# Attention's stores of x and the loads of the rests on ScalarE's queue, and raw bits of weight tiles 1 to 4 in the places of later tiles

## Chip, cores and metric

One core of a Trainium2 chip. The metric is the device time of one execution, in microseconds (us).

## The reference

Linear attention feeds a SwiGLU layer, and this a bilinear layer. Shapes: q, k and v are (4, 8, 576, 64); each layer has 2304 tokens, model width 512 and inner width 1536. All is float32.

```python
q_s = softmax(q, axis=-1)              # exp(q - max) / (sum + 1e-9)
k_s = softmax(k, axis=2)               # the same along the sequence
kv = np.einsum('bhsd,bhse->bhde', k_s, v)
x = np.einsum('bhsd,bhde->bhse', q_s, kv)   # then (B*S, H*D) = (2304, 512)
g = x @ w_gate
x = (g * sigmoid(g) * (x @ w_val)) @ w_out
x = ((x @ w_a) * (x @ w_b)) @ w_out2
```

## The kernel before

**Tiles.** Tokens go in five blocks: the first 512 positions of each of the four batches, and a fifth block with the 64 left over of each batch ("the rests"). The order is layer 0 with blocks 0, 1, 2, 4, 3, then layer 1 with blocks 0 to 4. The inner width is cut into NF = 12 tiles f. For each block and f there are two up products (`up`, lines 646 to 659; for the very first `ups`, line 639), the gate on ScalarE and VectorE (`gated`, lines 665 to 670) and the down product (`down`, lines 681 and 684). The down product of f - 1 comes after the up products of f.

**float32 in three passes.** Each operand is split in a high part, a cast to fp32r (ScalarE, line 293), and a low part, the difference (VectorE or GpSimd, line 287); three matmuls stand for one product.

**Weights.** Weights come as 64-bit numbers and are read as pairs of 32-bit words. A tile f of a layer has parts of the gate (or a), the value (or b) and the output matrix. `convert` loads the raw words of half a tile in three DMAs (lines 331 and 336) and turns them into float32: line 353 or 355, 357 (ScalarE, in place on the low words), 359, 362 and 365 (VectorE), 370 (GpSimd as a rule, the last that reads the raw words), then the split to the weight tile w. The raw words of a half tile are 6 KB in each partition; in layer 0 they have three places (`wr0`, `wr1`, `xraw`), in layer 1 two. Tile 0 is loaded by part instead of by half and uses the same three. Weight tile f of a layer lives in place `w{f}` of 12 KB in each partition; there are 12. Attention units of batches 0 and 1 use the places `w8` to `w11` for k, q and v until the weights of tiles 8 to 11 are written there.

**Attention.** `attend(b, g)` makes x for two heads of batch b (16 units). Batch 0 runs first; its rests come in six DMAs (`load_rests`, line 388). In batches 1 to 3 each unit loads its own rests (line 466). x of batch 0 stays in SBUF. For batches 1 to 3 x goes to DRAM: ScalarE copies it to `ob` (line 596) and SyncE stores it (line 597, 256 KB). The rests of all batches are copied (line 603) and stored as well (line 604, 32 KB). `next_x` (line 614) loads x again when its block comes.

**The order of the work.** All operations are put into a plan. It gives each a due time, counted back from TensorE's main line, and simulates the engines and the DMA queue with rough costs: at each step the operation that can start first goes next, and among those the one that is due first. The result is one order for each engine's queue. `load` chains all loads of inputs (`last_load`), so that they stand on SyncE's queue in the order of the program: start loads, weight tiles 1 and 2, attention unit (1, 0), tiles 3 and 4, unit (1, 1), and so on. An engine works its queue in order, so an instruction that waits holds all behind it. This is true of SyncE's DMAs too.

Of the kernel before, what the change touches and what calls it, by code (L numbers as in the profile page):

```python
# [9 lines left out]
U32 = mybir.dt.uint32  # L10
F32R = mybir.dt.float32r
AF = mybir.ActivationFunctionType
# [18 lines left out]
class Plan:  # L31
# [9 lines left out]
    BEGIN = 0.58  # L41
    SAME, HOP = 0.1, 0.17
    SLACK = 0.7
    DMA_START, DMA_END, DMA_RATE = 1.1, 0.95, 360e3
    TABLE = 1.3
    WINDOW = 10.24 / 3
    FAR = 1e9
# [47 lines left out]
    def prepare(self):  # L95

        ops = self.ops
        self.succ = [[] for _ in ops]
        for n, op in enumerate(ops):
            for d in op["deps"] | op["order"]:  # L100
                self.succ[d].append(n)
        self.due = [0.0] * len(ops)
        for n in reversed(range(len(ops))):
            op = ops[n]
            cost = op["cost"]
            if op["engine"] == "sync":
                cost += self.DMA_START + self.DMA_END + op["nbytes"] / self.DMA_RATE
            t = self.FAR
            for s in self.succ[n]:
                hop = self.hop(op["engine"], ops[s]["engine"], self.SLACK) if n in ops[s]["deps"] else 0.0  # L110
                t = min(t, self.due[s] - hop)
            t -= cost
            self.due[n] = t if op["wanted"] is None else min(t, op["wanted"])

    def order(self):


        ops, succ, due = self.ops, self.succ, self.due
# [31 lines left out]
        while len(done) < len(ops):  # L150
            best = None
            for engine, queue in ready.items():
                options = []
                for n, r in queue.items():
                    for b in ops[n]["allocs"]:
                        r = max(r, min(free_at(tag) for tag in b.tag))
                    if r < self.FAR and (ops[n]["engine"] == engine or better_here(n, r)):
                        options.append((max(r, port_at(n, engine)), n))
                if options:
                    t = max(free.get(engine, self.BEGIN), min(options)[0])  # L160
                    first = min((due[n], n) for r, n in options if r <= t + 0.02)
                    if best is None or (t, first) < best[:2]:
                        best = (t, first, engine, first[1])
            if best is None:
                raise RuntimeError("the plan is stuck")
            t, _, engine, n = best
            op = ops[n]
            for which, (e, *_) in enumerate(op["runs"]):
                del ready[e][n]
                if e == engine:  # L170
                    run[n] = which
            _, cost, _, port = op["runs"][run[n]]
            if port:
                port_free = t + cost
            for b in op["allocs"]:
                slot[b] = min(b.tag, key=free_at)
                holder[slot[b]] = b
            if op["table"] and op["table"] != table:
                table, t = op["table"], t + self.TABLE
            free[engine] = t + cost  # L180
            if engine == "sync":
                dma_free = max(dma_free, t + self.DMA_START) + op["nbytes"] / self.DMA_RATE
                end[n] = dma_free + self.DMA_END
            elif engine == "tensor":
                window = int(t / self.WINDOW)
                used[window] = used.get(window, 0.0) + cost
                full = used.get(window - 1, 0.0) > 0.3735 * self.WINDOW
                free[engine] = end[n] = t + cost * (1 if full else 2)
            else:
                end[n] = t + cost  # L190
            issued[n] = free[engine]
            done.append(n)
            for s in succ[n]:
                left[s] -= 1
                if not left[s]:
                    at = ops[s]["engine"]
                    is_ready(s, max([end[d] + self.hop(ops[d]["runs"][run[d]][0], at, self.HOP)
                                     for d in ops[s]["deps"]] + [issued[d] for d in ops[s]["order"]]))
# [13 lines left out]
def kernel(  # L212
# [24 lines left out]
    nc = tc.nc  # L237
    B, H, S, D = q.shape
    DM = H * D
    DFF = w_gate.shape[1]  # L240
    P = 128
    KD = DM // P
    NF = DFF // P
    R = 4
    SM = R * P
    SL = S - SM
# [5 lines left out]
    WC = 512  # L252

    const = ctx.enter_context(tc.tile_pool(name="const", bufs=1))
    wp = ctx.enter_context(tc.tile_pool(name="wp", bufs=1))
    xp = ctx.enter_context(tc.tile_pool(name="xp", bufs=1))
    hp = ctx.enter_context(tc.tile_pool(name="hp", bufs=2))
    sp = ctx.enter_context(tc.tile_pool(name="sp", bufs=2))
    op = ctx.enter_context(tc.tile_pool(name="op", bufs=2))
# [17 lines left out]
    def pool_us(n, streams=2):  # L277
        return (0, 0.14 + n / 1100, 0.15 + n / 449, 0.18 + n / 590)[streams]
# [14 lines left out]
        add("scalar", act_us(n), lambda: nc.scalar.copy(out=hi(), in_=src()), [src_key], [hi_key])  # L293
        pair(n, lo, src, lambda: hi().bitcast(F32), ALU.subtract, [src_key, hi_key], [lo_key], not psum, not psum)

    def dma(fn, nbytes, reads, writes, due=None, after=(), issue=0.475):
        return add("sync", issue, fn, reads, writes, due=due, nbytes=nbytes, after=after)


    last_load, last_x = [], []  # L300
# [1 line left out]
    def load(fn, nbytes, writes, issue=0.475):  # L302
        n = dma(fn, nbytes, [], writes, after=last_load, issue=issue)
        last_load[:] = [n]
# [3 lines left out]
    w_t, w_parts = {}, {}  # L308
    WR, AT = ("wr0", "wr1"), ("a0", "a1", "a2")
    RAW = WR + ("xraw",)  # L310
    TOP = 122880.0
    LEAST = 2.0 ** -15

    def convert(l, f, c, ms, c0, c1, spare):


        n, width = len(ms), c1 - c0
        name = f"{l}_{f}_{c}"
        raw = Buf(sp, [P, n, width, 2], U32, RAW if spare else WR, f"wr{name}")
        a = Buf(sp, [P, n, width], U32, AT, f"a{name}")  # L320
        if (l, f) not in w_t:
            w_t[l, f] = Buf(wp, [P, 6, WC], F32R, f"w{f}", f"w{l}_{f}")
            w_parts[l, f] = {m: [] for m in range(3)}
        w = w_t[l, f]
        parts = [(raw, x) for x in range(n)]
        for x, m in enumerate(ms):
            w_parts[l, f][m].append(c)

            def get(x=x, m=m):
                if m < 2:  # L330
                    nc.sync.dma_start(  # L331
                        out=raw()[:, x].rearrange("p (c n) t -> p c (n t)", n=P),
                        in_=mats[l][m][:, f * 2 * P:(f + 1) * 2 * P].rearrange(
                            "(c p) n -> p c n", p=P)[:, c0 // P:c1 // P, :])
                else:
                    nc.sync.dma_start(
                        out=raw()[:, x].rearrange("p n t -> p (n t)"),
                        in_=mats[l][m][f * P:(f + 1) * P, 2 * c0:2 * c1])

            load(get, P * width * 8, [(raw, x)])  # L340

        def low():
            return raw()[:, :, :, 0]

        def high():
            return raw()[:, :, :, 1]

        def part(t):
            return w().rearrange("p (m t) n -> p m t n", t=2)[:, ms[0]:ms[-1] + 1, t, c0:c1]
# [5 lines left out]
            other=("vector", dve_us(e, 2), lambda: nc.vector.tensor_scalar(  # L355
                out=a(), in0=high(), scalar1=0x7FFFFFFF, scalar2=None, op0=ALU.bitwise_and), True))
        add("scalar", act_us(e) + 0.08, lambda: nc.scalar.activation(  # L357
            out=low(), in_=low(), func=AF.Copy, scale=2.0 ** -29), parts, [(raw, "low")])
        add("vector", dve_us(e, 2), lambda: nc.vector.tensor_scalar(  # L359
            out=a().bitcast(F32), in0=a().bitcast(F32), scalar1=TOP, scalar2=LEAST,  # L360
            op0=ALU.min, op1=ALU.max), [a], [a], port=True)
# [7 lines left out]
        def whole(engine):  # L369
            engine.tensor_tensor(out=a(), in0=a(), in1=low(), op=ALU.add)  # L370

        add("gpsimd", pool_us(e), lambda: whole(nc.gpsimd), [a, (raw, "low")], [a],
            other=("vector", dve_us(e), lambda: whole(nc.vector), True))
        split(lambda: part(0), lambda: part(1), lambda: a().bitcast(F32), e, (w, (c, 0)), (w, (c, 1)), a)

    def convert_tile(l, f):
        for h in range(2):
            spare = l == 0 and f < NF - 2
            list(convert(l, f, h, [0, 1, 2], h * WC // 2, (h + 1) * WC // 2, spare))


    def rest(h):
# [2 lines left out]
    def load_rests(b, src, at):  # L385

        for h in range(HG):
            load(lambda h=h: nc.sync.dma_start(
                out=rests()[rest(h), at],
                in_=src[b, :, SM:S, :].rearrange("(g h) s d -> h s g d", h=HG)[h]),  # L390
                SL * KD * D * 8, [(rests, (at, h))], issue=0.65)

    def attend(b, g, xhl, due):

# [196 lines left out]
        if xhl is not None:  # L591
            split(lambda: xhl()[:, 0, g, :], lambda: xhl()[:, 1, g, :], px, SM,
                  (xhl, (0, g)), (xhl, (1, g)), px, psum=True)
        else:
            ob = Buf(op, [P, 512], F32, ("ob0", "ob1"), f"xs{u}")
            add("scalar", act_us(SM), lambda: nc.scalar.copy(out=ob(), in_=px()), [px], [ob])
            dma(lambda: nc.sync.dma_start(out=xd[0][b]()[:, g, :], in_=ob()), P * SM * 4,
                [ob], [(xd[0][b], g)])
        add("tensor", mm_us(SL), lambda: nc.tensor.matmul(
            py(), lhsT=kvbd(), rhs=qT()[:, SM:S], start=True, stop=True), [QTL, *BDS], [py],  # L600
            due=None if due is None else due + 1)
        oc = Buf(op, [P, 512], F32, ("ob0", "ob1"), f"xq{u}")
        add("scalar", act_us(SL), lambda: nc.scalar.copy(out=oc()[:, 0:SL], in_=py()), [py], [oc])
        dma(lambda: nc.sync.dma_start(out=xd[0][B]()[:, g, b * SL:(b + 1) * SL], in_=oc()[:, 0:SL]),
            P * SL * 8, [oc], [(xd[0][B], (g, b))])


    def new_xhl(l, i):
# [194 lines left out]
```

## Time and profile before

| | us |
|---|---|
| median of 3 runs | 1038.8 |
| lowest and highest | 1037.66, 1039.71 |
| profiled execution | 1037.9 |
| its span from the first to the last instruction | 1036.0 |

| engine | busy, us | share of the span |
|---|---|---|
| TensorE, matmuls | 977.9 | 94% |
| VectorE | 431.8 | 42% |
| ScalarE | 357.7 | 35% |
| GpSimd | 178.2 | 17% |

In the profile PE is TensorE, PEld its loading of weights, DVE VectorE, ACT ScalarE, POOL GpSimd, and SPq SyncE's queue, which issues DMAs. L331 is line 331 of the kernel. Names of tiles stand as output<-input, without their numbers. Shares of the whole span are means over stages that differ: the first 200 us, where weights are converted and batch 1 goes through attention beside the first block, and the rest.

### The profile page before, as it was taken

To read this page: it belongs to the slowest core of one execution; us is meant where nothing else is said; L and a number is where in the kernel's file an instruction comes from. 1 tells how busy PE (TensorE), PEld (TensorE's weight loads), DVE (VectorE), ACT (ScalarE), POOL (GpSimd) and SP (SyncE) were. 2 spreads that over 40 slices of the span, in tenths; PEclk is the share of its full clock that TensorE was granted. 3 is DMA by queue.
4 is the path that set the end of the run, shared out by engine and by line. 5 is a ranking of instruction groups with operands and counts; after the bars stand their busy time and mean duration, and the time that the engine had idled before them with its cause. 6 is when DMAs were issued, how large, how long until landed. Compare 5 with 4: busy or idle time off the path is not lost.

```text
span 1036.0 us, 12377 instructions
## 1 busy us (share of the span) xinstructions
PE 977.9 (94%) x4792; PEld 797.4 (77%) x4792; DVE 431.8 (42%) x758; ACT 357.7 (35%) x574; POOL 178.2 (17%) x156
## 2 busy tenths in 40 slices
PE   4777879999999999999999999999999999999997
PEld 3455656677778777799888788888888888888897
DVE  5876688633334333432665774131113112111211
ACT  4556565432334323422355543121112112111211
POOL 4543444301110101100145443000000000000000
PEclk9989989999999999999999999999999999999999
DMA  6445543311121111521133531020002000100100
GB/s 198 120 134 168 168 149 111 117 56 47 47 69 59 46 46 46 175 92 61 62 123 122 194 108 54 1 82 1 1 1 82 1 1 0 61 1 1 41 1 22
DMA packets 63876, 74.22 MB, mean 72 GB/s; under 512 B 12616, under 2 KB 51016, under 8 KB 62920
## 3 DMA queue, kind: packets, MB, share of 16 engines
q1 hardware_dynamic: 63816, 73.42, 22.4%
q8 instruction: 38, 0.62, 0.3%
q14 instruction: 22, 0.18, 0.1%
HBM read 60.29 MB, written 13.11 MB: 71 GB/s over the span
## 4 chain that ended last, share of the span: by engine, by line
PE 80%; DMA 6%; DVE 5%; SPq 3%; issue 2%; ACT 2%; POOL 2%; DVEq 0%; POOLq 0%; ACTq 0%
PE u L654 51%; PE acc L684 14%; PE acc L681 11%; DMA wr<-in_moe_w_out_dram 3%; PE kv L544 2%; POOL a L370 1%; DVE a L365 1%; SPq L331 1%; DVE h L287 1%; SPq L461 1%; PE xt L589 1%; PE kv L546 1%; PE qt L574 1%; DMA ut<-in_v_dram 1%; DMA x<-ob 1%
## 5 line engine op out<-in xcount | busy, mean ns | idle before, releaser
L654 PE MATMUL u<-xhl,w 128*128 128x512 f32 (+1 forms) x2856 | 621.9, 372 | 14.8 <-DVE w L287 12.6
L654 PEld LDWEIGHTS u<-xhl,w 128*128 128x128 f32 x2856 | 497.0, 189 | 110.6 <-DVE w L287 11.7
L668 DVE TENSOR_TENSOR s<-s,u 128x512 f32<-128x512 f32 (+1 forms) x120 | 76.1, 634 | 395.1 <-PE u L654 382.7
L681 PE MATMUL acc<-h,w 128*128 128x512 f32 (+1 forms) x720 | 167.6, 379 | 12.5 <-DVE h L287 10.7
L681 PEld LDWEIGHTS acc<-h,w 128*128 128x128 f32 x720 | 125.5, 190 | 42.3 <-DVE h L287 14.4
L684 PE MATMUL acc<-w,h 128*128 128x512 f32 x648 | 157.5, 391 | 0.1
L665 ACT ACTIVATE s<-u 128x512 f32<-128x512 f32 (+1 forms) x120 | 66.6, 555 | 262.0 <-PE u L654 255.2
L684 PEld LDWEIGHTS acc<-w,h 128*128 128x128 f32 x648 | 120.7, 188 | 26.2 <-DVE h L287 1.3
L293 ACT CAST h<-s 128x512 fp32r<-128x512 f32 (+1 forms) x120 | 69.1, 576 | 205.0 <-DVE s L668 204.7
L370 POOL TENSOR_TENSOR a<-a,wr 128x768 uint32<-128x768 uint32 (+1 forms) x49 | 99.4, 2033 | 205.0 <-DVE a L365 141.4
L287 DVE TENSOR_TENSOR h<-s,h 128x512 fp32r<-128x512 f32 (+1 forms) x119 | 84.3, 709 | 51.5 <-ACT h L293 51.3
L287 POOL TENSOR_TENSOR xhl<-xraw,xhl 128x512 fp32r<-128x512 f32 (+1 forms) x5 | 6.0, 1202 | 337.9 <-ACT xhl L293 240.9
L365 DVE SCALAR_TENSOR_TENSOR a<-wr,a 128x768 uint32<-128x768 uint32 (+1 forms) x49 | 52.4, 1077 | 0.5
L353 ACT ACTIVATE a<-wr 128x768 f32<-128x768 f32 (+1 forms) x38 | 33.7, 888 | 45.0 <-DMA wr<-in_moe_w_out_dram 34.9
L293 ACT CAST w<-a 128x768 fp32r<-128x768 f32 (+1 forms) x49 | 39.9, 818 | 23.2 <-POOL a L370 19.8
L357 ACT ACTIVATE wr<-wr 128x768 uint32<-128x768 uint32 (+1 forms) x49 | 43.8, 893 | 10.3 <-DMA wr<-in_moe_w_out_dram 10.3
L359 DVE TENSOR_SCALAR a<-a 128x768 f32<-128x768 f32 (+1 forms) x49 | 36.0, 739 | 18.8 <-ACT a L353 18.3
L287 DVE TENSOR_TENSOR w<-a,w 128x768 fp32r<-128x768 f32 (+1 forms) x38 | 38.3, 1021 | 8.5 <-ACT w L293 8.5
L567 POOL TENSOR_TENSOR ua<-ua,st 128x576 f32<-128x576 f32 x8 | 9.2, 1154 | 122.4 <-DVE st L566 122.4
L362 DVE TENSOR_SCALAR a<-a 128x768 uint32<-128x768 uint32 (+1 forms) x49 | 27.6, 572 | 0.8
L287 POOL TENSOR_TENSOR w<-a,w 128x768 fp32r<-128x768 f32 (+1 forms) x11 | 22.9, 2080 | 19.6 <-ACT w L293 19.6
L697 DVE COPY ob<-acc 128x512 f32<-128x512 f32 (+1 forms) x20 | 12.7, 636 | 27.9 <-DMA out_dram<-ob 19.9
(94 smaller groups left out, 439.2 us busy)
## 6 DMA issues: line engine op xcount, KB each, us to landing
wr<-in_moe_w_out_dram SPq DMA_DIRECT2D x46, 256.0 KB
xraw<-x SPq DMA_DIRECT2D x7, 1024.0 KB
wr<-in_moe_w_a_dram SPq DMA_DIRECT2D x24, 256.0 KB
wr<-in_moe_w_b_dram SPq DMA_DIRECT2D x24, 256.0 KB
wr<-in_moe_w_gate_dram SPq DMA_DIRECT2D x22, 256.0 KB
wr<-in_moe_w_val_dram SPq DMA_DIRECT2D x22, 256.0 KB
x<-ob SPq DMA_DIRECT2D x16, 256.0 KB
out_dram<-ob SPq DMA_DIRECT2D x16, 256.0 KB
```

Of the source, the lines that this page charges most:

```text
L287: engine.tensor_tensor(out=out(), in0=x(), in1=y(), op=op)
L293: add("scalar", act_us(n), lambda: nc.scalar.copy(out=hi(), in_=src()), [src_key], [hi_key])
L353: add("scalar", act_us(e) + 0.08, lambda: nc.scalar.activation(out=a().bitcast(F32), in_=high().bitcast(F32), func=AF.Abs), parts, [a], ot ...
L357: add("scalar", act_us(e) + 0.08, lambda: nc.scalar.activation(out=low(), in_=low(), func=AF.Copy, scale=2.0 ** -29), parts, [(raw, "low")])
L359: add("vector", dve_us(e, 2), lambda: nc.vector.tensor_scalar(out=a().bitcast(F32), in0=a().bitcast(F32), scalar1=TOP, scalar2=LEAST, op0= ...
L365: add("vector", dve_us(e), lambda: nc.vector.scalar_tensor_tensor(out=a(), in0=high(), scalar=0xC0000000, in1=a(), op0=ALU.bitwise_and, op ...
L370: engine.tensor_tensor(out=a(), in0=a(), in1=low(), op=ALU.add)
L654: nc.tensor.matmul(ps()[:, 0:n], lhsT=wv[:, c, :], rhs=x()[:, xs, c, 0:n], start=(a == 0 and c == 0), stop=(a == 2 and c == KD - 1))
L665: add("scalar", act_us(n), lambda: nc.scalar.activation(out=s()[:, 0:n], in_=ga()[:, 0:n], func=AF.Silu if l == 0 else AF.Copy), [ga], [s] ...
L668: add("vector", dve_us(n), lambda: nc.vector.tensor_tensor(out=s()[:, 0:n], in0=s()[:, 0:n], in1=gb()[:, 0:n], op=ALU.mult), [s, gb], [s])
L681: nc.tensor.matmul(ps()[:, 0:n], lhsT=w()[:, 4 + ws, o * P:(o + 1) * P], rhs=h()[:, hs, 0:n], start=begin, stop=end)
L684: nc.tensor.matmul(ps(), lhsT=h()[:, hs, o * P:(o + 1) * P], rhs=w()[:, 4 + ws, :], start=begin, stop=end)
```

## The change

Three things. The stores of lines 597 and 604 and the six loads of the rests of line 388 are issued by ScalarE instead of SyncE; the loads of the rests leave the chain of loads. The raw words of weight tiles 1 to 4 of layer 0, both halves of a tile together, get 12 KB of their own: the places `w4` to `w7` of the weight tiles 4 to 7, which are written later. The three shared places serve tiles 0 and 5 to 9 then (tiles 10 and 11 had and have two). And the plan counts a DMA's time for every operation that moves bytes, on whichever queue, at a rate of 300 instead of 360 GB/s.

```diff
-    DMA_START, DMA_END, DMA_RATE = 1.1, 0.95, 360e3
+    DMA_START, DMA_END, DMA_RATE = 1.1, 0.95, 300e3
...
-            if op["engine"] == "sync":
+            if op["nbytes"]:
                 cost += self.DMA_START + self.DMA_END + op["nbytes"] / self.DMA_RATE
...
-            if engine == "sync":
+            if op["nbytes"]:
                 dma_free = max(dma_free, t + self.DMA_START) + op["nbytes"] / self.DMA_RATE
...
-    def dma(fn, nbytes, reads, writes, due=None, after=(), issue=0.475):
-        return add("sync", issue, fn, reads, writes, due=due, nbytes=nbytes, after=after)
+    def dma(fn, nbytes, reads, writes, due=None, after=(), issue=0.475, queue="sync"):
+        return add(queue, issue, fn, reads, writes, due=due, nbytes=nbytes, after=after)
...
+    AHEAD = 4
...
-        raw = Buf(sp, [P, n, width, 2], U32, RAW if spare else WR, f"wr{name}")
+        if raw is None:
+            raw, rows, h = Buf(sp, [P, n, width, 2], U32, RAW if spare else WR, f"wr{name}"), (lambda: raw()), 0
+        else:
+            rows, h = (lambda: raw()[:, c]), c
...
     def convert_tile(l, f):
+        spare, raw = l == 0 and f < NF - 2, None
+        if l == 0 and f <= AHEAD:
+            raw = Buf(wp, [P, 2, 3, WC // 2, 2], U32, f"w{f + NF - KD - AHEAD - 1}", f"wr{l}_{f}")
         for h in range(2):
-            spare = l == 0 and f < NF - 2
-            list(convert(l, f, h, [0, 1, 2], h * WC // 2, (h + 1) * WC // 2, spare))
+            list(convert(l, f, h, [0, 1, 2], h * WC // 2, (h + 1) * WC // 2, spare, raw))
...
-            load(lambda h=h: nc.sync.dma_start(
+            dma(lambda h=h: nc.scalar.dma_start(
                 out=rests()[rest(h), at],
                 in_=src[b, :, SM:S, :].rearrange("(g h) s d -> h s g d", h=HG)[h]),
-                SL * KD * D * 8, [(rests, (at, h))], issue=0.65)
+                SL * KD * D * 8, [], [(rests, (at, h))], issue=0.65, queue="scalar")
...
-            dma(lambda: nc.sync.dma_start(out=xd[0][b]()[:, g, :], in_=ob()), P * SM * 4,
-                [ob], [(xd[0][b], g)])
+            dma(lambda: nc.scalar.dma_start(out=xd[0][b]()[:, g, :], in_=ob()), P * SM * 4,
+                [ob], [(xd[0][b], g)], queue="scalar")
...
-        dma(lambda: nc.sync.dma_start(out=xd[0][B]()[:, g, b * SL:(b + 1) * SL], in_=oc()[:, 0:SL]),
-            P * SL * 8, [oc], [(xd[0][B], (g, b))])
+        dma(lambda: nc.scalar.dma_start(out=xd[0][B]()[:, g, b * SL:(b + 1) * SL], in_=oc()[:, 0:SL]),
+            P * SL * 8, [oc], [(xd[0][B], (g, b))], queue="scalar")
```

## Rows read from the trace of the kernel before

**Rows 1.** Busy us by stretch and engine (instructions), granted clock, DMA share, GB/s.

```profile
30.00:60.00 30.00, 16.63 (x93) 10.85 (x92) 24.24 (x43) 17.11 (x29) 16.29 (x14) 0.89 0.55 164
60.00:100.00 40.00, 34.34 (x148) 25.46 (x149) 29.81 (x54) 25.03 (x34) 16.21 (x12) 0.93 0.47 150
100.00:150.00 50.00, 39.77 (x184) 29.95 (x183) 37.39 (x62) 28.11 (x38) 21.94 (x17) 0.92 0.49 152
150.00:200.00 50.00, 46.18 (x211) 33.45 (x210) 40.03 (x67) 27.56 (x43) 19.50 (x15) 1.00 0.36 114
200.00:420.00 220.00, 220.00 (x1087) 174.17 (x1087) 78.19 (x183) 76.73 (x120) 20.53 (x36) 1.00 0.17 53
```

The columns of rows 1 and 5 are: stretch, its length, then PE, PEld, DVE, ACT, POOL.

**Rows 2.** TensorE's timeline: start, us, instructions; in brackets idle time before and its releaser.

```profile
45.54 5.60 PE L639 MATMUL u<-xhl,w 128*128 128x512 f32 x21 [0.41 <-DVE w L287]
...
59.94 2.93 PE L654 MATMUL u<-xhl,w 128*128 128x512 f32 x6 [7.52 <-DVE w L287]
...
83.74 5.78 PE L654 MATMUL u<-xhl,w 128*128 128x512 f32 x24 [1.22 <-ACT s L665]
...
96.14 0.70 PE L654 MATMUL u<-xhl,w 128*128 128x512 f32 x2 [3.23 <-DVE w L287]
...
116.88 1.12 PE L589 MATMUL xt<-ut 128*128 128x512 f32 x2 [2.93 <-ACT ut L583]
...
124.50 5.62 PE L654 MATMUL u<-xhl,w 128*128 128x512 f32 x24
...
136.81 0.80 PE L681 MATMUL acc<-h,w 128*128 128x512 f32 x1 [5.96 <-DVE h L287]
```

**Rows 3.** SyncE's waits, 0 to 200 us: total us, times, longest us.

```profile
SPq L331 <- POOL a L370: 73.7, 16, 12.6
SPq L604 <- ACT xq L603: 17.0, 2, 15.1
...
SPq L597 <- ACT xq L603: 7.6, 2, 6.0
```

**Rows 4.** SyncE's timeline: start, us of issue, DMAs.

```profile
2.27 1.41 SPq L388 DMA_DIRECT2D rests<-in_k_dram  x2
...
29.92 0.82 SPq L604 DMA_DIRECT2D x<-xq  x2
36.35 0.38 SPq L331 DMA_DIRECT2D wr<-in_moe_w_gate_dram  x1
...
122.04 0.40 SPq L331 DMA_DIRECT2D wr<-in_moe_w_gate_dram  x1
```

**Rows 5.** Stretches as in rows 1, for the DMA share.

```profile
5.00:10.00 5.00, 1.31 (x3) 0.55 (x3) 3.04 (x9) 0.96 (x2) 1.06 (x1) 1.00 0.88 235
10.00:15.00 5.00, 0.48 (x1) 0.18 (x1) 4.96 (x13) 2.30 (x8) 3.08 (x5) 1.00 0.96 310
26.00:36.00 10.00, 7.30 (x50) 4.53 (x49) 7.91 (x22) 5.84 (x13) 3.34 (x4) 1.00 0.04 8
```

**Rows 6.** ScalarE's timeline: steps that waited for loads.

```profile
41.23 0.89 ACT L353 ACTIVATE a<-wr 128x768 f32<-128x768 f32 x1 [4.26 <-DMA wr<-in_moe_w_out_dram]
...
91.17 0.91 ACT L353 ACTIVATE a<-wr 128x768 f32<-128x768 f32 x1 [2.36 <-DMA wr<-in_moe_w_out_dram]
...
115.72 0.62 ACT L486 COPY ut<-ut 128x512 f32<-128x512 f32 x1 [2.96 <-DMA ut<-in_v_dram]
...
127.84 0.89 ACT L353 ACTIVATE a<-wr 128x768 f32<-128x768 f32 x1 [4.66 <-DMA wr<-in_moe_w_out_dram]
```

**Rows 7.** VectorE's timeline at tile 1's second half.

```profile
56.46 0.69 DVE L519 TENSOR_REDUCE st<-ut 128x8 f32<-128x512 f32 x1 [3.42 <-DMA ut<-in_q_dram]
...
58.94 0.95 DVE L287 TENSOR_TENSOR w<-a,w 128x768 fp32r<-128x768 f32 x1
```

**Rows 8.** SyncE's small stores: issue in ns, least, median and most.

```profile
L604 SPq DMA_DIRECT2D x<-xq x16: 320/378/2167, 29.9 to 421.7; - x16
```

**Rows 9.** The page's group of GpSimd's adds: busy us, mean ns of one, idle before.

```profile
L370 POOL TENSOR_TENSOR a<-a,wr 128x768 uint32<-128x768 uint32 (+1 forms) x49 | 99.4, 2033 | 205.0 <-DVE a L365 141.4
```

More of the change, by code (lines that the diff above doesn't have):

```diff
@@ L310, with convert @@
     RAW = WR + ("xraw",)
+    AHEAD = 4
     TOP = 122880.0
     LEAST = 2.0 ** -15
-    def convert(l, f, c, ms, c0, c1, spare):
+    def convert(l, f, c, ms, c0, c1, spare, raw=None):
         n, width = len(ms), c1 - c0
         name = f"{l}_{f}_{c}"
-        raw = Buf(sp, [P, n, width, 2], U32, RAW if spare else WR, f"wr{name}")
+        if raw is None:
+            raw, rows, h = Buf(sp, [P, n, width, 2], U32, RAW if spare else WR, f"wr{name}"), (lambda: raw()), 0
+        else:
+            rows, h = (lambda: raw()[:, c]), c
         a = Buf(sp, [P, n, width], U32, AT, f"a{name}")
@@ L324, in convert @@
         w = w_t[l, f]
-        parts = [(raw, x) for x in range(n)]
+        parts = [(raw, (h, x)) for x in range(n)]
         for x, m in enumerate(ms):
@@ L331, in get @@
                     nc.sync.dma_start(
-                        out=raw()[:, x].rearrange("p (c n) t -> p c (n t)", n=P),
+                        out=rows()[:, x].rearrange("p (c n) t -> p c (n t)", n=P),
                         in_=mats[l][m][:, f * 2 * P:(f + 1) * 2 * P].rearrange(
@@ L336, in get @@
                     nc.sync.dma_start(
-                        out=raw()[:, x].rearrange("p n t -> p (n t)"),
+                        out=rows()[:, x].rearrange("p n t -> p (n t)"),
                         in_=mats[l][m][f * P:(f + 1) * P, 2 * c0:2 * c1])
-            load(get, P * width * 8, [(raw, x)])
+            load(get, P * width * 8, [(raw, (h, x))])
         def low():
-            return raw()[:, :, :, 0]
+            return rows()[:, :, :, 0]
         def high():
-            return raw()[:, :, :, 1]
+            return rows()[:, :, :, 1]
         def part(t):
@@ L357, in convert @@
         add("scalar", act_us(e) + 0.08, lambda: nc.scalar.activation(
-            out=low(), in_=low(), func=AF.Copy, scale=2.0 ** -29), parts, [(raw, "low")])
+            out=low(), in_=low(), func=AF.Copy, scale=2.0 ** -29), parts, [(raw, (h, "low"))])
         add("vector", dve_us(e, 2), lambda: nc.vector.tensor_scalar(
@@ L370, in whole @@
             engine.tensor_tensor(out=a(), in0=a(), in1=low(), op=ALU.add)
-        add("gpsimd", pool_us(e), lambda: whole(nc.gpsimd), [a, (raw, "low")], [a],
+        add("gpsimd", pool_us(e), lambda: whole(nc.gpsimd), [a, (raw, (h, "low"))], [a],
             other=("vector", dve_us(e), lambda: whole(nc.vector), True))
```

## Prediction

> **What bounds the kernel now.** I read the busy time by stretch first [rows 1]. Before 30 us there is the start; it is taken up below. From 200 us to 420 us TensorE is busy for 220.00 of 220 us: there only TensorE's own work counts, and no load or store that comes sooner can be felt. Between 30 and 200 us, the first block of tokens of layer 0, TensorE is busy 16.63 + 34.34 + 39.77 + 46.18 = 136.9 of 170 us. So 33.1 us are open there, 29.3 of them before 150 us. VectorE has 24.24 + 29.81 + 37.39 + 40.03 = 131.5 us of work in the same 170 us, 77%; no engine is full, and the granted clock is 0.89 to 0.93 up to 150 us.
>
> TensorE's timeline says where the idle time lies [rows 2]. In brackets stands the wait before a group. The largest are 7.52 us before tile 1's first matmuls at 59.94, 3.23 us before tile 4's at 96.14, 2.93 us in attention at 116.88, 5.96 us at 136.81, where the down product of tile 6 starts, and 1.22 us at 83.74. Together 20.9 us. Each longer stall is followed by matmuls at about half the rate: the row at 124.50 gives 5.62/24 = 0.234 us for one; after the stall at 59.94 six take 2.93 us, 1.5 us over; at 96.14 two take 0.70 us instead of 0.47.
>
> Then the question what made VectorE and ScalarE late. SyncE's waits [rows 3] say that its loads of weights waited 73.7 us in 16 waits for the GpSimd add that frees a raw place (three places for all 6 KB half tiles), 17.0 us for ScalarE behind a small store, and 7.6 us behind a large one. SyncE's timeline [rows 4] shows the worst: two small stores go out at 29.92, the first after a wait of 15.1 us [rows 3], and tile 1's first load at 36.35, so that nothing was issued from about 15 to 30 us. In 26 to 36 us the DMA engines are 0.04 busy [rows 5], while VectorE will wait for precisely these bits. ScalarE, whose queue is in order, sits 4.26 us until tile 1's bits land, 2.36 us and 4.66 us for later weights, and 2.96 us for v of an attention unit [rows 6]. VectorE waits 3.42 us at 56.46 for that unit's q, with tile 1's last step only at 58.94 behind it [rows 7].
>
> **The change part by part.**
>
> *Raw places.* Tiles 1 to 4 get 12 KB each in the places of tiles 4 to 7. Those are empty at the start, so the 8 half tiles (24 DMAs) no longer wait for a GpSimd add; SyncE can issue tile 1 and 2 right behind the start loads, by about 17 us. The first attention unit of the second batch stands behind tile 2 in load order and needs a tile of the first batch to be done; the two small stores at 29.92 are the last work of two of these, so tiles 3 and 4 follow from there. At the 310 GB/s of 10 to 15 us [rows 5], 6.3 MB are 20 us of transfers, so I estimate that all four tiles are in by 45 us; before, tile 1 alone landed at 41.2. The three shared places are then free for tiles 5 and 6. From tile 7 on the loads are again three half tiles ahead of conversion, as now.
>
> The 7.52 us stall: its last step is VectorE's, and VectorE is 24.24/30 = 81% busy in that stretch, with 5.76 us free, 3.42 of them the wait for q, which is now loaded earlier. So 3.4 us at least and 7.5 at most; I take 5.5. Tile 4 and the wait ahead of it, 1.22 + 3.23 = 4.5 us: ScalarE's 2.36 us wait for bits of tile 5 stands in front of the gate there. Ends 0 and 4.5; I take 3, somewhat more than that wait, since tile 4's own bits are early too. The 2.93 us at 116.88: v of a later unit, whose load stands behind tile 6's second half and so still behind a freed place; ends 0 and 2.9, I take 1.
>
> *Stores off SyncE.* What a store waits for on SyncE, all later loads wait for. The 15 us wait up to 29.92 gives nothing by itself in the old layout, since the next load would then wait for its place till 36.35; with the new places it would cost nearly the whole advance, so it is part of the 5.5 us. The longest wait of a large store, 6.0 us [rows 3], ends at 121; the load at 122.04 behind it has no wait of its own, ScalarE then waits 4.66 us for it at 127.84, and the 5.96 us stall follows. Ends 0 and 6; I take 3, because the place was free only for part of these 6 us at best.
>
> *Clock.* The slow matmuls after the three stalls, have two prices here: 1.5 us behind 7.52 us of waiting, and 0.2 us in the two matmuls shown behind 3.23 us. At the first price, 1.5/7.52 = 0.2 us for each us of waiting, the 16.7 us of the three long stalls cost 3.3 us, and the rate stays low for longer than the six matmuls counted, as the granted clock of 0.89 in 30 us and 0.93 and 0.92 after says: (0.11 x 30) + (0.07 x 40) + (0.08 x 50) = 10 us at most, some of it idle. With most of the waiting gone I take 3 back (0 to 10).
>
> *Start.* Six loads of rests leave SyncE: 1.41 us for two, three such pairs, some 4 us of issue ahead of v [rows 4]. ScalarE computes for 0.96 of the 5 us from 5 to 10 us, so issuing there costs nothing. But the DMA engines are 0.88 and 0.96 busy from 5 to 10 and 10 to 15 us [rows 5], and the bytes are the same: 0 to 4 us, and I take 0.5, near the DMA row. The Trainium skill ("DMA: Bandwidth & Descriptors", section "Issuing engines are not separate DMA queues") says that DMAs from different engines interleave on the same 16 DMA engines and that issuing from several saves only the sequencer's time; by that the start would be worth at most its issue time, and the stores too. The row at 0.96 agrees for the start, which would lower the sum by 0.5; for the stores the rule leaves out what rows 3 show, a queue held by a waiting instruction.
>
> *Costs.* ScalarE now issues stores: 4 large and 8 small ones in the first 200 us. A small store took 378 ns in the median on SyncE and 2167 at most [rows 8], so 12 stores are 4.5 us, at most 26 us, on an engine that is 55 to 57% busy [rows 1]. Queued behind them are the gate and the casts of weights and h, for which VectorE and TensorE wait. Each store also waits for ScalarE's own copy just ahead. Most lies in ScalarE's idle time; I take 1 us (0 to 5). After 200 us the other 16 stores lie beside a full TensorE: nothing.
>
> Conversions of tiles 1 and 2 can now start while the first batch's attention is still a chain of short steps on all engines (TensorE's long run of tile 0, 21 matmuls, starts at 45.54 [rows 2]). An engine that has begun a step finishes it: 2.03 us of GpSimd [rows 9] or 0.9 us of ScalarE [rows 6]. I take 3 us of delay, some three or four such collisions on the path (0 to 10). The new planning rate and costing of stores reorder steps everywhere; I put that at nothing and into the range.
>
> Sum: 0.5 + 5.5 + 3 + 1 + 3 + 3 - 1 - 3 = 12.0 us. The profiled execution had 1037.9 us (span 1036.0) and the median of the runs is 1038.8, 0.9 above it: 1025.9 for the profiled one and **1026.8** for the median. Check against the next bound: with 12 us gone VectorE's 131.5 us fill 83% of 158 us; it reached 81% in the first 30 us of the stretch, so this is possible but near what it does in the best part. At 88% the stretch would be 149 us, 21 us gained; I take that as the most, 1018.
>
> **The rivals.**
>
> VectorE takes over. The prefetched bits pile up before an engine that was nearly full anyway, and later stalls stay. For it: 81% busy up to 60 us, and from tile 7 on the loads are no further ahead than now. Against it: its waits on DMA and on ScalarE behind DMA. Then only tile 1's 5.5 us and a clock gain of 1.5 come, less 2 of costs: 5 us, 1034.
>
> All stalls go. Conversions run a tile ahead and no load is waited for before tile 8. For it: 20.9 us of waits in few places, almost each with a DMA in its chain. 20 us, 1019.
>
> Slower. First-batch attention is hurt by conversions that start too early: TensorE's block 0 cannot start before x's four column groups are there (45.5 us). If a GpSimd add of 2.03 us or a ScalarE step of 0.9 us falls in front of ten or more of the chain's steps, the start moves back by over 15 us, and the stalls behind it then are worth less than the delay. It decides from about 15 us of delay on; with 20 us it gives 1044. Against it: the planner ranks by due time, and attention of the first batch is due first.
>
> Nothing changes. SyncE still stands in front of the attention loads behind tile 2 until their place is free, and tile 1's conversion is anyway late: 1038.5. The DMA idle time of 15 us speaks against it.
>
> By the Trainium skill's rule above alone this last case would come out; the chance of this case is that of the rule.
>
> **How the numbers follow.** Forecast (1021 to 1031) 0.48; VectorE takes over 0.22; all stalls go 0.15; slower 0.10; nothing 0.05. About 0.2%, 2 us, is what a measurement of this kernel can tell from no change. Faster: 0.48 + 0.22 + 0.15 = 0.85; same 0.05; slower 0.10. The range takes in the forecast, the VectorE case with its scatter up to 1037, and most of the case in which all stalls go, down to 1016.
>
> **What would show it.** Right: tile 1's first load issued near 14 us and the fourth tile's last before 45 us; DMA engines busy in 20 to 36 us; ScalarE's wait at 41 us gone; the stall before tile 1's matmuls under 2 us; VectorE over 80% busy from 30 to 150 us; TensorE without a gap from about 188 us on instead of 200, and nothing changed behind that. Wrong: first matmuls of block 0 later than now by several us (the slower rival); the stall before tile 1 gone but equal stalls with VectorE as releaser later (VectorE takes over); long DMA issues on ScalarE in front of gates; a stall at the start of the second block, because its x comes later than the faster first block needs it.

## The result and the profile after

| | before | after |
|---|---|---|
| median, us | 1039.26 (4 runs, 1037.66 to 1041.15) | 1027.3 (4 runs, 1025.0 to 1028.91) |
| ratio, 95% interval | | 0.9883 (0.9854 to 0.9911) |
| profiled execution, us | 1037.9 | 1026.0 |
| its span, us | 1036.0 | 1024.2 |

The change makes the kernel 12.0 us faster; the interval of the ratio is 9 to 15 us. The sum of the forecast came out at the same number. Its terms did not, and that is what the experiments are about.

Busy time by stretch in the kernel after, columns as in [rows 1]:

```profile
30.00:60.00 30.00, 22.45 (x101) 16.02 (x102) 25.20 (x48) 20.95 (x37) 17.49 (x15) 0.74 0.72 225
60.00:100.00 40.00, 35.24 (x162) 26.11 (x161) 36.56 (x55) 23.82 (x31) 21.07 (x14) 0.98 0.07 22
100.00:150.00 50.00, 44.61 (x213) 32.97 (x212) 42.09 (x67) 33.85 (x49) 23.59 (x16) 0.97 0.52 164
150.00:200.00 50.00, 46.53 (x228) 35.25 (x226) 36.63 (x65) 27.14 (x39) 17.68 (x15) 1.00 0.35 114
200.00:420.00 220.00, 220.00 (x1076) 174.24 (x1075) 75.56 (x176) 75.91 (x125) 19.84 (x36) 1.00 0.20 59
```

Between 30 and 200 us TensorE is busy 148.8 us instead of 136.9. VectorE is the engine to look at: from 30 to 100 us it is busy for 25.20 + 36.56 = 61.8 us, against 24.24 + 29.81 = 54.1 before [rows 1]. From 45 to 70 us it is full, first line after, second line before:

```profile
45.00:70.00 25.00, 17.84 (x63) 12.42 (x61) 24.77 (x33) 17.65 (x26) 15.87 (x9) 0.86 0.43 135
```

```profile
45.00:70.00 25.00, 16.70 (x62) 12.71 (x62) 19.28 (x28) 16.40 (x23) 11.93 (x9) 0.83 0.57 171
```

Busy is not the same as done. Some of VectorE's steps take longer than before: here is the remainder of a half weight tile from 30 to 100 us, after and then before (count, busy us, mean ns of one):

```profile
L287 DVE TENSOR_TENSOR w<-a,w 128x768 fp32r<-128x768 f32 x8 | 11.6, 1469 | 0.6 <-ACT w L293 0.6
```

```profile
L287 DVE TENSOR_TENSOR w<-a,w 128x768 fp32r<-128x768 f32 x7 | 6.6, 964 | 1.7 <-ACT w L293 1.7
```

So 5.0 of the 7.7 us more lie in these steps, with one step more.

SyncE's timeline after, to be read against [rows 4]:

```profile
13.82 0.37 SPq L336 DMA_DIRECT2D wr<-in_moe_w_gate_dram  x1
...
22.60 0.34 SPq L341 DMA_DIRECT2D wr<-in_moe_w_out_dram  x1
...
40.82 0.34 SPq L341 DMA_DIRECT2D wr<-in_moe_w_out_dram  x1
...
55.27 0.98 SPq L341 DMA_DIRECT2D wr<-in_moe_w_out_dram  x1
97.19 0.37 SPq L336 DMA_DIRECT2D wr<-in_moe_w_gate_dram  x1
```

Tile 1's first load goes out at 13.82 instead of 36.35, tile 2's last at 22.60, tile 4's last at 40.82. The three shared places are filled again by 55.27, and then no weight is loaded until 97.19: for 40 us the kernel lives on what it has, with the DMA engines 0.07 busy.

TensorE's timeline after:

```profile
44.90 3.99 PE L646 MATMUL u<-xhl,w 128*128 128x512 f32 x15
...
54.33 0.95 PE L661 MATMUL u<-xhl,w 128*128 128x512 f32 x2 [3.83 <-DVE w L287]
56.07 2.93 PE L661 MATMUL u<-xhl,w 128*128 128x512 f32 x6 [0.79 <-DVE w L287]
...
66.80 2.59 PE L688 MATMUL acc<-h,w 128*128 128x512 f32 x10 [1.51 <-DVE h L287]
70.41 0.68 PE L551 MATMUL kv<-ut 128*64 128x65 f32 x8 [1.02 <-ACT ut L541]
...
82.71 2.88 PE L661 MATMUL u<-xhl,w 128*128 128x512 f32 x12
...
91.49 0.65 PE L661 MATMUL u<-xhl,w 128*128 128x512 f32 x2
...
97.83 0.63 PE L688 MATMUL acc<-h,w 128*128 128x512 f32 x2
...
102.13 0.68 PE L551 MATMUL kv<-ut 128*64 128x65 f32 x8
...
114.78 2.96 PE L688 MATMUL acc<-h,w 128*128 128x512 f32 x12
117.58 5.62 PE L661 MATMUL u<-xhl,w 128*128 128x512 f32 x24
...
126.02 0.52 PE L688 MATMUL acc<-h,w 128*128 128x512 f32 x1 [2.37 <-DVE h L287]
...
130.53 5.63 PE L661 MATMUL u<-xhl,w 128*128 128x512 f32 x24
...
142.61 5.83 PE L661 MATMUL u<-xhl,w 128*128 128x512 f32 x24
...
177.68 5.28 PE L661 MATMUL u<-xhl,w 128*128 128x512 f32 x22 [0.74 <-DVE w L287]
...
188.58 5.73 PE L661 MATMUL u<-xhl,w 128*128 128x512 f32 x24
```

Five more lines of the kernel before, for the same pieces of work as those at 102.13, 97.83, 114.78, 130.53 and 188.58:

```profile
105.05 0.68 PE L544 MATMUL kv<-ut 128*64 128x65 f32 x8 [0.23 <-ACT ut L534]
...
106.78 0.73 PE L681 MATMUL acc<-h,w 128*128 128x512 f32 x2
...
121.70 2.96 PE L681 MATMUL acc<-h,w 128*128 128x512 f32 x12
...
141.67 5.98 PE L654 MATMUL u<-xhl,w 128*128 128x512 f32 x24
...
200.76 5.73 PE L654 MATMUL u<-xhl,w 128*128 128x512 f32 x24
```

So the lead over the kernel before can be read at each piece. At tile 3's up product it is 83.74 - 82.71 = 1.0 us [rows 2]; at tile 4's 96.14 - 91.49 = 4.7; at tile 4's down product 121.70 - 114.78 = 6.9, and the same at tile 6's up product (124.50 - 117.58); at tile 7's 141.67 - 130.53 = 11.1; at the start of the second block 200.76 - 188.58 = 12.2. From there on little is gained or lost: the spans differ by 11.8. At each of these pieces both kernels have done the same work. At tile 3's down product (106.78 and 97.83) they have not: the kernel before has done an attention unit's kv matmuls by then (from 105.05), the changed kernel takes them up behind it (at 102.13), so the 9.0 us between these two times are no lead.

ScalarE issues the stores without visible harm; issue in ns, least, median and most, to be read against [rows 8]:

```profile
L611 ACTq DMA_DIRECT2D x<-xq x16: 326/342/1397, 32.2 to 409.5; - x16
```

### The profile page after: what moved, and what is told of

Read it like the earlier page. It is cut to its first block, busy times and chain, and to the rows that moved or that the text cites. A ratio compares the mean times of both kernels' runs of the same rounds, so it can differ in the third digit from the quotient of the medians.

```text
span 1024.2 us, 12303 instructions
## 1 busy us (share of the span) xinstructions
PE 980.6 (96%) x4792; PEld 800.1 (78%) x4792; DVE 435.8 (43%) x751; ACT 361.2 (35%) x579; POOL 179.6 (18%) x158
## 4 chain that ended last, share of the span: by engine, by line
PE 85%; DVE 5%; DMA 3%; ACT 2%; issue 2%; POOL 2%; SPq 1%; ACTq 0%; DVEq 0%; POOLq 0%
PE u L661 54%; PE acc L691 14%; PE acc L688 12%; PE kv L551 2%; DMA ut<-in_k_dram 1%; DVE w L287 1%; DVE a L370 1%; PE xt L596 1%; PE qt L581 1%; PE kv L553 1%; POOL a L375 1%; DVE h L287 1%; DMA ut<-in_q_dram 1%; DVE a L367 0%; DMA wr<-in_moe_w_out_dram 0%
## 5 line engine op out<-in xcount | busy, mean ns | idle before, releaser
L375 POOL TENSOR_TENSOR a<-a,wr 128x768 uint32<-128x768 uint32 (+1 forms) x48 | 95.8, 2000 | 189.6 <-DVE a L370 142.0
L370 DVE SCALAR_TENSOR_TENSOR a<-wr,a 128x768 uint32<-128x768 uint32 (+1 forms) x49 | 57.2, 1174 | 0.7 <-DVE s L675 0.2
L358 ACT ACTIVATE a<-wr 128x768 f32<-128x768 f32 (+1 forms) x43 | 38.2, 892 | 27.9 <-DMA wr<-in_moe_w_out_dram 25.5
L287 DVE TENSOR_TENSOR w<-a,w 128x768 fp32r<-128x768 f32 (+1 forms) x38 | 41.9, 1113 | 6.0 <-ACT w L293 5.8
L364 DVE TENSOR_SCALAR a<-a 128x768 f32<-128x768 f32 (+1 forms) x49 | 32.6, 672 | 15.0 <-ACT a L358 14.7
L367 DVE TENSOR_SCALAR a<-a 128x768 uint32<-128x768 uint32 (+1 forms) x49 | 29.8, 618 | 0.7
L287 POOL TENSOR_TENSOR w<-a,w 128x768 fp32r<-128x768 f32 (+1 forms) x11 | 20.7, 1885 | 19.1 <-ACT w L293 19.1
L293 ACT CAST xhl<-xraw 128x512 fp32r<-128x512 f32 (+1 forms) x36 | 18.6, 569 | 11.9 <-PE u L661 11.8
```

Of the source, the lines that this page charges most:

```text
L287: engine.tensor_tensor(out=out(), in0=x(), in1=y(), op=op)
L370: add("vector", dve_us(e), lambda: nc.vector.scalar_tensor_tensor(out=a(), in0=high(), scalar=0xC0000000, in1=a(), op0=ALU.bitwise_and, op ...
```

## The experiments

Each was timed in three rounds beside the kernel before, on the same chip; ratios are to that. Except where it is said, the plan makes a new order for each kernel. Leads are read from the profiled execution of each, which lies up to 3.5 us from its median.

**Which part carries the gain.** Stores and rests back on SyncE, raw places kept:

```diff
-            dma(lambda h=h: nc.scalar.dma_start(
+            load(lambda h=h: nc.sync.dma_start(
...
-            dma(lambda: nc.scalar.dma_start(out=xd[0][b]()[:, g, :], in_=ob()), P * SM * 4,
-                [ob], [(xd[0][b], g)], queue="scalar")
+            dma(lambda: nc.sync.dma_start(out=xd[0][b]()[:, g, :], in_=ob()), P * SM * 4,
+                [ob], [(xd[0][b], g)])
```

(and the small store in the same way)

> The changed kernel with stores and rests back on SyncE; tiles 1 to 4 keep their own raw places, the order is planned anew. Theory (loads that no longer wait for a freed place carry the gain; the stores matter only where they hold loads): 1030 to 1035, that is half or more of the 12 us. Rival (the move off SyncE's queue carries it): 1036 or more.

Measured: 1026.76 us, ratio 0.9884 (0.985 to 0.9919). All of the gain, more than was expected. Why the stores on SyncE's queue did no harm stands in its timeline:

```profile
47.94 0.47 SPq L341 DMA_DIRECT2D wr<-in_moe_w_out_dram  x1
48.51 0.85 SPq L611 DMA_DIRECT2D x<-xq  x2
56.93 0.39 SPq L336 DMA_DIRECT2D wr<-in_moe_w_gate_dram  x1
```

Once the loads have places, the plan puts them all ahead of the first store, down to tile 5. The store comes at 48.51 and holds nothing that is wanted.

The other half alone, no raw places ahead:

```diff
-    AHEAD = 4
+    AHEAD = 0
```

> The changed kernel with no raw places ahead (three shared places for all tiles, as before); stores and rests on ScalarE. Theory: 1034 to 1038, the first loads still wait for a freed place until about 36 us. Rival (queues carry it): 1027 to 1031.

Measured: 1035.6 us, ratio 0.9972 (0.9956 to 0.9988). By the ratio 3 us, and the order alone may give 2 of them, as the next run shows: the planned rate alone.

```diff
-    DMA_START, DMA_END, DMA_RATE = 1.1, 0.95, 360e3
+    DMA_START, DMA_END, DMA_RATE = 1.1, 0.95, 300e3
```

> The kernel before with only the planned DMA rate changed, 300 for 360 GB/s: nothing but the order of instructions differs. Theory: 1036 to 1043, no change that means anything. Rival (the gain is a luckier order): below 1033.

Measured: 1037.89 us, ratio 0.9978 (0.9959 to 0.9998). The intervals of these two lie on each other, so in the whole time the move off SyncE's queue has no gain of its own that was measured here.

The changed kernel with the old rate:

```diff
-    DMA_START, DMA_END, DMA_RATE = 1.1, 0.95, 300e3
+    DMA_START, DMA_END, DMA_RATE = 1.1, 0.95, 360e3
```

> The changed kernel with the planned DMA rate of before, 360 for 300 GB/s; only the order differs. Theory (the rate is worth no more than the scatter between orders): 1024 to 1031. Rival (the rate carries part of the gain): 1033 or more.

Measured: 1031.32 us, ratio 0.9918 (0.9888 to 0.9947), just above what was expected. The intervals of this and the changed kernel overlap; the rate may be worth up to some 4 us, by the order that it happens to make. What differs by less than that between two kernels with orders of their own is not put down to the edit below.

**What an order of its own can cost.** At tile 7's up product, which the kernel before starts at 141.67, the changed kernel has a lead of 11.1 us. The kernel with the new rate alone starts it at 135.99, a lead of 5.7 us. The kernel with the stores off SyncE and no places ahead has 11.9 us, and loses most of it behind, where TensorE waits for VectorE's last step on the weights of tiles 8 and 11:

```profile
129.81 0.69 PE L661 MATMUL u<-xhl,w 128*128 128x512 f32 x2
...
149.48 8.18 PE L661 MATMUL u<-xhl,w 128*128 128x512 f32 x22 [3.41 <-DVE w L287]
...
184.74 5.28 PE L661 MATMUL u<-xhl,w 128*128 128x512 f32 x22 [3.05 <-DVE w L287]
```

In the changed kernel tile 8's up product runs through (142.61), and the wait at tile 11 is 0.74 us. No run here separates whether these late waits come from the missing places or from the order that the plan happened to make. By whole times the places carry the gain: the four kernels that differ only in the issuing engine or the planned rate and have tiles 1 to 4 ahead gain 8 to 12 us by their ratios (0.9883, 0.9884, 0.9918, and 0.991 in the next run), the two without places 2 to 3.

**A store's queue at equal order.** The plan and all orders of the changed kernel, but the stores issued by SyncE at the same point of the program:

```diff
-            dma(lambda: nc.scalar.dma_start(out=xd[0][b]()[:, g, :], in_=ob()), P * SM * 4,
+            dma(lambda: nc.sync.dma_start(out=xd[0][b]()[:, g, :], in_=ob()), P * SM * 4,
                 [ob], [(xd[0][b], g)], queue="scalar")
```

(and the small store)

> The changed kernel's order exactly, but the stores of x are issued by SyncE at the same point of the program order; TensorE, VectorE and GpSimd have the same queues. Theory: loads behind a waiting store are late again, 1030 to 1036. Rival (a store's queue does not matter once places are there, or ScalarE's issue time costs as much): 1025 to 1029.

Measured: 1029.73 us, ratio 0.991 (0.9879 to 0.9941). Between the two expectations, and its interval overlaps that of the changed kernel: 2.4 us at most likely, not settled. Even here the first store goes out at 35.96, when 20 of the 24 loads of tiles 1 to 4 are issued.

**How many tiles ahead.**

```diff
-    AHEAD = 4
+    AHEAD = 2
```

> The changed kernel with own raw places for tiles 1 and 2 alone. Its trace shows the lead over the kernel before at the down product of tile 0 as 0.9 us, none at tile 2, 6.8 us from tile 4 on, 11.2 us at the down product of tile 5. Theory (the lead comes where tiles 3 and 4 no longer wait for a place): 1031 to 1035. Rival (the first tiles' loads carry it): 1025 to 1029.

Measured: 1033.2 us, ratio 0.995 (0.9934 to 0.9966), the theory's time. Tile 4's second half is loaded at

```profile
76.53 0.37 SPq L336 DMA_DIRECT2D wr<-in_moe_w_gate_dram  x1
```

and TensorE begins tile 4's up product at 96.16, where the kernel before begins it at 96.14 [rows 2] and the changed kernel at 91.49. But that is not where the time is lost. At tile 4's down product, with the same work done, this kernel starts at 115.90 and leads the kernel before by 5.8 us, at tile 7's up product by 141.67 - 131.72 = 10.0. The rest goes at tiles 8 and 11 again:

```profile
131.72 6.02 PE L661 MATMUL u<-xhl,w 128*128 128x512 f32 x24
...
149.38 7.35 PE L661 MATMUL u<-xhl,w 128*128 128x512 f32 x22 [4.47 <-DVE w L287]
...
184.64 6.82 PE L661 MATMUL u<-xhl,w 128*128 128x512 f32 x22 [3.52 <-DVE w L287]
```

Tile 8's last half was issued from 125.01 on, 24 us before the first of these waits, so this wait is not for its load. The places of tiles 3 and 4 give some 5 us at tile 4's up product; whether the 6 us of the whole time are theirs or the order's stays open.

```diff
-    AHEAD = 4
+    AHEAD = 6
```

> The changed kernel with own raw places for tiles 1 to 6. Theory (from tile 7 on loads are late again: ScalarE still waits 7.7 us for weights between 30 and 200 us): another 2 to 5 us, 1022 to 1025. Rival (VectorE has taken over, 91% busy from 60 to 100 us): 1026 to 1030.

Measured: 1029.63 us, ratio 0.9921 (0.9897 to 0.9945). The rival's time: two more tiles ahead brought nothing here. Tile 4's up product starts at 92.43, a microsecond later than with four tiles.

**What ate the gain at tile 1.** First theory: conversions that start early stand in front of other steps. ScalarE's scaling of the low words is held back until the first step on the same half tile is done:

```diff
         add("scalar", act_us(e) + 0.08, lambda: nc.scalar.activation(
-            out=low(), in_=low(), func=AF.Copy, scale=2.0 ** -29), parts, [(raw, (h, "low"))])
+            out=low(), in_=low(), func=AF.Copy, scale=2.0 ** -29), [*parts, a], [(raw, (h, "low"))])
```

> The changed kernel, but ScalarE's scaling of a half tile's low words (0.9 us) waits for the first step on the high words, so that it no longer runs ahead: eleven such steps stand before 62 us in the changed kernel. Theory (early conversions stand in front of the first batch's attention and of tile 1's casts, and ate the gain that was forecast at tile 1): 1022 to 1025, with tile 1's up product starting by 52 us instead of 54.3. Rival (VectorE and GpSimd set that place): 1026 to 1030, tile 1 as before.

Measured: 1033.39 us, ratio 0.9955 (0.9938 to 0.9972), slower than both had it. Only four of the scalings now stand before 62 us instead of eleven. Tile 1's up product does start earlier, at 52.59 instead of 54.33, but at tile 4's down product the lead is 121.70 - 119.73 = 2.0 us instead of 6.9, and the kernel is 6 us slower. So the theory falls as an account of the time: what the held scalings gave at tile 1 was lost again by tile 4.

The same from the other side, all conversions of tiles 1 to 11 planned behind the first batch's x:

```diff
+    hold = []
...
-            out=a().bitcast(F32), in_=high().bitcast(F32), func=AF.Abs), parts, [a],
+            out=a().bitcast(F32), in_=high().bitcast(F32), func=AF.Abs), parts, [a], after=hold,
...
-            out=low(), in_=low(), func=AF.Copy, scale=2.0 ** -29), parts, [(raw, (h, "low"))])
+            out=low(), in_=low(), func=AF.Copy, scale=2.0 ** -29), parts, [(raw, (h, "low"))], after=hold)
...
+    hold[:] = xhl.users
     for f in range(1, NF):
```

> The changed kernel, with ScalarE's two first steps of every conversion of tiles 1 to 11 planned behind the last step of the first batch's x; loads as in the changed kernel. Theory (VectorE sets the pace, so its early idle time is worth using): 1029 to 1035. Rival (early conversions delay the first batch's attention): 1021 to 1025, tile 0's up products ending before 48 us instead of 50.5.

Measured: 1035.22 us, ratio 0.9962 (0.9945 to 0.9978), the theory's time. But the run does not decide. Tile 0's up products are not earlier but later, after a wait for ScalarE's copy xq, and on ScalarE that copy stands behind seven of the held scalings. ScalarE's line first, then TensorE's two waits:

```profile
46.74 5.65 ACT L363 ACTIVATE wr<-wr 128x768 uint32<-128x768 uint32 x7
```

```profile
54.25 7.56 PE L647 MATMUL u<-xhl,w 128*128 128x512 f32 x21 [7.85 <-ACT xq L611]
...
183.91 7.85 PE L662 MATMUL u<-xhl,w 128*128 128x512 f32 x22 [5.20 <-DVE w L287]
```

So the edit itself put conversions in front of the first batch's last steps, which is the rival's own mechanism. And the delay is made good: this kernel starts tile 7's up product at 131.79, a lead of 9.9 us, and loses most of it at the wait before tile 11's. What early conversions are worth stays open.

Second theory: GpSimd's adds and VectorE slow each other at tile 1. The adds of tile 1 go to VectorE:

```diff
-        add("gpsimd", pool_us(e), lambda: whole(nc.gpsimd), [a, (raw, (h, "low"))], [a],
-            other=("vector", dve_us(e), lambda: whole(nc.vector), True))
+        if l == 0 and f == 1:
+            add("vector", dve_us(e), lambda: whole(nc.vector), [a, (raw, (h, "low"))], [a], port=True)
+        else:
+            add("gpsimd", pool_us(e), lambda: whole(nc.gpsimd), [a, (raw, (h, "low"))], [a],
+                other=("vector", dve_us(e), lambda: whole(nc.vector), True))
```

> The changed kernel, with tile 1's two adds of low and high words on VectorE (about 1 us each) instead of GpSimd (2 us each, beside which VectorE's steps in the trace are stretched: two casts' remainders take 3.77 us instead of 1.9). Theory (the two engines slow each other at tile 1): tile 1's up product 2 us or more earlier than 54.3, 1023 to 1026. Rival (the later stages absorb it, or VectorE is short of time anyway): 1026 to 1031.

Measured: 1026.73 us, ratio 0.989 (0.9865 to 0.9915): no difference, the rival's time. Tile 1's up product starts at 55.86, later than 54.33 and not earlier. The adds are now VectorE's work there, so the run does not show what the two engines cost each other. What holds tile 1 stays open.

**Is VectorE the bound?** The clamp of each weight conversion of layer 0's tiles 1 to 11 is left out, in both kernels:

```diff
-        add("vector", dve_us(e, 2), lambda: nc.vector.tensor_scalar(
-            out=a().bitcast(F32), in0=a().bitcast(F32), scalar1=TOP, scalar2=LEAST,
-            op0=ALU.min, op1=ALU.max), [a], [a], port=True)
+        if l == 1 or f == 0:
+            add("vector", dve_us(e, 2), lambda: nc.vector.tensor_scalar(
+                out=a().bitcast(F32), in0=a().bitcast(F32), scalar1=TOP, scalar2=LEAST,
+                op0=ALU.min, op1=ALU.max), [a], [a], port=True)
```

> The changed kernel without the clamp of line 364 for layer 0's tiles 1 to 11: 22 VectorE steps of 0.55 us, 12.2 us less work for VectorE, 10 of them before 100 us; all else as in the changed kernel, the order planned anew. Theory (with the loads ahead VectorE sets the pace up to 100 us; it is 99% busy from 45 to 70 us): 5 to 9 us faster than the changed kernel, 1018 to 1022. Rival (another engine or the chain between them sets it): 1024 or more.

Measured: 1015.41 us, ratio 0.9765 (0.9736 to 0.9794). 11.9 us faster than the changed kernel, for 12.2 us of VectorE's work: about one for one, more than the theory's band. At tile 4's down product 114.78 - 107.70 = 7.1 us of it are there.

> The kernel before without the same clamp (line 359), 12 us less work for VectorE. Theory (there the loads set the pace, VectorE has gaps): 0 to 4 us faster than before, 1035 to 1039. Rival (VectorE was the bound before, too, and the raw places helped in another way): 1026 to 1032.

Measured: 1020.72 us, ratio 0.9816 (0.9783 to 0.9849). 17 us faster than before, beyond even the rival's band. The theory that loads alone set the pace before, and that VectorE's gaps left its work without weight, falls. One line of SyncE's waits, 0 to 200 us, against the first of [rows 3]:

```profile
SPq L331 <- POOL a L371: 50.1, 13, 9.0
```

A shorter conversion frees its raw place sooner, and the waits for a place drop from 73.7 to 50.1 us. In the kernel before, a load waits for a conversion and the conversion for VectorE, in one loop, so VectorE's steps and the loads' times add up. That is the reading which fits; since the order was planned anew, how much of the 17 us is the loop and how much the order stays open. A rival is left in both kernels: the clamp is a step in each conversion's chain as well as work for VectorE, and no run gives VectorE less work, or more, outside this chain.

## Why the prediction was right, and where its steps were not

*The sum* was 12.0 us and 12 us came: the raw places were the right place to look, and the loads came when forecast (tile 1 near 14 us, tile 4 issued before 45).

Of the signs, tile 1's wait of under 2 us did not come; VectorE's 25.20 + 36.56 + 42.09 = 103.9 us from 30 to 150 us, 87%, and the second block from 188 us on did.

*Start*, 0.5 us: TensorE's first long run of attention begins at 15.92 instead of 16.29, 0.4 us. Right.

*Tile 1*, 5.5 us: this step failed. The six matmuls start 59.94 - 56.07 = 3.9 us earlier, but the stall is not gone (3.83 and 0.79 us), and new waits for VectorE and ScalarE follow (1.51 and 1.02). At tile 3's up product only 1.0 us of lead is left. The step said that VectorE had 5.76 us free in this stretch; that time is used up, as the 24.77 of 25 us from 45 to 70 us show, in part by steps that take longer. The rival in which VectorE takes over describes this stretch. The price of 3 us for early conversions is not seen at tile 0: the long run of its up products starts at 44.90 instead of 45.54, although its first three matmuls come at 43.00 instead of 38.37. (Two readings were loose: two matmuls of tile 1's up product ran at 51.68, ahead of the six at 59.94, and what landed by 41.2 was half of tile 1.)

*Tile 4*, 3 us, and *v at 116.88*, 1 us: mis-sized; the lead grows by 5.9 us, from 1.0 at tile 3's up product to 4.7 at tile 4's and 6.9 at tile 4's down product. The waits of 3.23 us before tile 4 and of 2.93 us for v are gone. The prediction gave most to the longest stall, at tile 1; the gain comes at the next two, here and at 136.81.

*The stall at 136.81*, 3 us: 2.37 instead of 5.96 us, and the lead grows by 4.2 us to tile 7. The reason given, a store that holds SyncE's queue, did not carry it: with the stores on SyncE and the raw places kept, the kernel is as fast. The order has a part in it: with the planned rate alone, tile 6's up product starts at 121.53 and tile 7's at 135.99, so that the lead grows there from 3.0 to 5.7 us. From tile 7 to the second block another 1.1 us come, for which the forecast had no term.

*Stores off SyncE*: the sentence that they would cost nearly the whole advance failed. The prediction took the order on SyncE's queue as given; the plan makes a new one, and puts the early loads ahead of the stores. The Trainium skill ("DMA: Bandwidth & Descriptors", section "Issuing engines are not separate DMA queues") says that issue from another engine saves only issue time. The whole times agree with that (0.9972 beside 0.9978 for the rate alone); the leads at tile 7, 11.9 and 5.7 us, leave it open.

*Clock*, 3 us back: from 30 to 60 us the mean granted clock fell from 0.89 to 0.74, and from 60 to 150 us it rose to 0.98 and 0.97 from 0.93 and 0.92. 0.15 of 30 us against 0.05 of 90 us: nothing on balance, by the mean over busy and idle time alike.

*Costs on ScalarE*, 1 us: the median issue of a small store is 342 ns; no run shows a loss. (ScalarE was 63% busy from 60 to 100 us before, 25.03 of 40 us, and not 55 to 57%.)

So errors cancelled: too much at tile 1 and for the clock, too little at tile 4, at 136.81 and behind tile 7. That the sum met the measured time is luck: the same change with the old planned rate has 1031.3 us, 4 us from it. And the view of [rows 1] misled in one point: VectorE at 77% was not an engine with room, as the runs without the clamp show. That its gaps were waits inside a loop of which it was a part is the reading that fits.

## What to carry to other kernels

When a stage waits for a buffer that a conversion has to free, count the loop of load, conversion and release as one path: more places or a shorter conversion both help, and work taken off an engine in that loop can shorten the whole although the engine is only 77% busy. Do not look for the gain of a prefetch at the longest stall alone; read the lead at several pieces of work, and only where both kernels have done the same work. When a planner makes a new order for each variant, a difference of a few us between two variants can be the order's. Before a store is moved to another queue for the loads behind it, see whether it stands in front of them once they can be issued early.

## What the runs showed of the hardware

VectorE's steps are stretched beside GpSimd more than I had reckoned. One remainder of a half tile took 0.95 us [rows 7]; in the kernel after, two of them took 3.77 us while GpSimd worked through the last of three adds and a subtraction (both timelines, VectorE's line first):

```profile
52.24 3.77 DVE L287 TENSOR_TENSOR w<-a,w 128x768 fp32r<-128x768 f32 x2
```

```profile
47.45 6.02 POOL L375 TENSOR_TENSOR a<-a,wr 128x768 uint32<-128x768 uint32 x3 [5.77 <-DMA ut<-in_q_dram]
53.42 1.77 POOL L531 TENSOR_TENSOR ut<-ut,st 128x512 f32<-128x512 f32 x1
```

The Trainium skill ("SBUF — State Buffer", section "SBUF: two separate sides") says that the two engines share a pair of ports, and that where VectorE's instruction has two inputs in SBUF, as here, the one that starts first holds the pair to its end while the other waits. The lines agree with that: VectorE's pair ends at 52.24 + 3.77 = 56.01, 0.8 us behind the subtraction's end at 53.42 + 1.77 = 55.19, about the time of one step alone. What such waits cost the whole no run shows: moving tile 1's adds to VectorE brought nothing, but made them VectorE's own work.

TensorE's clock fell in a stretch in which it was busy, after it had waited 2.05 us at 33 us: from 35 to 45 us the granted clock is near the lower of its two levels, 1.2 of 2.4 GHz. The matching five-microsecond stretches before had 1.00 and 0.83.

```profile
35.00:40.00 5.00, 4.97 (x29) 3.96 (x30) 2.86 (x7) 4.16 (x8) 4.58 (x6) 0.50 0.76 233
40.00:45.00 5.00, 5.00 (x18) 3.07 (x16) 2.85 (x10) 2.81 (x4) 1.67 (x2) 0.56 1.00 336
```
